# Seven block products in place of eight for the first product of the second layer of an FFT filter, expert and feed-forward kernel

## The chip, the core and the metric

The kernel runs on one core of one Trainium2 chip. Its time is the device time of one execution in microseconds. The kernel before took 3979.79 us, the median of 3 runs (3979.67 to 3984.19).

Five engines work side by side, each through its own list of instructions in order: TensorE (PE in the profile, with PEld for the loading of its stationary operand), VectorE (DVE), ScalarE (ACT), GpSimd (POOL) and SyncE (SP, which here only issues DMAs). They wait for each other by semaphores. Matrix products are written to PSUM, eight banks of 128 x 512 fp32 values, and the other engines read them from there.

## The reference

Three stages follow each other. The first filters `x` (8 batches x 3072 positions x 256 channels) along the positions in the frequency domain. The second sends each of the 24576 tokens through one of 8 experts. The third, the second layer of this document, is a feed-forward layer over all tokens, with `w_in` of 256 x 2048 and `w_out` of 2048 x 256:

```python
def _moe2_ref(x, w_in, w_out) -> np.ndarray:
    h = x @ w_in
    g = h * (1.0 / (1.0 + np.exp(-1.702 * h)))
    return (g @ w_out).astype(np.float32)
```

## The kernel before

The change lies in the last stage, behind `c2.close()`. It works through `nblk` = 48 blocks of 512 tokens. For a block, `load_z` gathers four tiles of 128 tokens x 256 channels by indirect DMAs that POOL issues, `scale_z` multiplies them by a gate value for each token on DVE, and `prep_z` turns them (TensorE transposes, helper `split_t`, L568), so that channels lie on the partitions. The result is split into two fp32r numbers: `xh` is the rounded value (an ACT cast, L573), `xl` the rest (a DVE subtraction, L574). The weights were split in the same way before: `wm[0]`, `wm[1]` (tiles winh, winl) hold `w_in`, and `wm[2]`, `wm[3]` (wouth, woutl) hold `w_out`.

A product of two split matrices is three matmuls: high x high, high x low, low x high. A step `t` of the main loop handles one strip of 128 of the 2048 hidden values of one block:

1. `gemm1` (L583): 6 matmuls 128x128 by 128x512 (two halves of the 256 channels, three each) into one PSUM bank of the pool `ph`, which has four banks.
2. ACT computes the sigmoid of the bank into `sig` (L975), DVE multiplies it with the bank into `gg` (L976).
3. One step later ACT casts `gg` to `hh` (L968) and DVE subtracts to get `hl` (L969).
4. Two steps later `gemm2` (L592) multiplies this strip by its 128 rows of `w_out`: 4 tiles of 128 tokens x 3 matmuls of 256 columns, added up in four PSUM tiles `pz` over the 16 strips of a block.

After strip 15 ACT copies the four `pz` tiles to `zo` (L990) and SP stores them. `load_z` of the block after next stands in step 4 of a block, `scale_z` of the next block in step 8, `prep_z` in steps 9 and 11.

The order is the program's own (`manual_schedule`): each engine executes its instructions in the order in which the Python code writes them, and a pool's buffers decide what has to be waited for. The three lines that set the path of a strip are

```python
                S.copy(hh, gg)
                V.tensor_tensor(hl, gg, hh.bitcast(F32), op=ALU.subtract)
        ...
                p = gemm1(wm[0], wm[1], *xt[j], f, 512)
```

Of the kernel before, what the change touches and what calls it, by code (L numbers as in the profile page):

```python
# [124 lines left out]
def fftconv_moe_moe2(ctx: ExitStack, tc: tile.TileContext, x, ffl, fny, wg, w1, w2, win, wout,  # L125
                     t_sq, t_m2, t_m3, t_sg, t_sm, out):
    nc = tc.nc
# [417 lines left out]

    def open_expert_pools():
        op = lambda n, bufs, **k: tc.tile_pool(name=n, bufs=bufs, reuse_waits="tile", **k)
        pools["xt"] = ctx.enter_context(op("xtp", 2))
        pools["ph"] = ctx.enter_context(op("php", 4, space=PSUM))
        pools["raw"] = c2.enter_context(op("rawp", 1))  # L550
        pools["we"] = c2.enter_context(op("wep", 2))
        pools["m"] = c2.enter_context(op("mp", 2))

# [10 lines left out]
    def split_t(xg, nt, k):  # L564

        p = pools["ph"].tile([128, 4, 128], F32, name="ph", tag="ph")
        for c in range(nt):
            T.transpose(p[:, c, :], xg[:, c, 128 * k:128 * k + 128], eye)  # L568
        return p
# [23 lines left out]
                n += 1  # L593

    def pz_tiles(nt, first):
        return [pools["pz"].tile([128, D], F32, name="pz", tag=f"pz{first + c}") for c in range(nt)]

    raw, wt, xg, xt = {}, {}, {}, {}

# [317 lines left out]
    c2.close()  # L917


    with ExitStack() as c3:  # L920
        gp2 = c3.enter_context(tc.tile_pool(name="gp2", bufs=2, reuse_waits="tile"))
        zg, xt = {}, {}
        nblk = NTOK // 512

        def load_z(j):
# [10 lines left out]
        def scale_z(j):  # L936
            if j >= nblk:
                return
            for c in range(4):
                o = 4 * j + c  # L940
                V.tensor_scalar(zg[j][:, c, :], zg[j][:, c, :], s_all[:, o:o + 1], None, op0=ALU.mult)  # L941

        def prep_z(j, k):
            if j >= nblk:
                return
            if k == 0:
                xt[j] = [pools["xt"].tile([128, 2, 512], F32R, name="xh"), pools["xt"].tile([128, 2, 512], F32R, name="xl")]
            p = split_t(zg[j], 4, k)
            split_out(p, 4, *xt[j], k)
            if k == 1:  # L950
# [5 lines left out]
        scale_z(0)  # L956
        load_z(1)
        prep_z(0, 0)
        prep_z(0, 1)
        gq, hq, pz = {}, {}, {}  # L960
        ns = 16 * nblk
        for t in range(ns + 2):
            j, f = divmod(t, 16)
            if t - 1 in gq:
                gg = gq.pop(t - 1)
                hh = gp2.tile([128, 512], F32R, name="hh", bufs=3)
                hl = gp2.tile([128, 512], F32R, name="hl", bufs=3)
                S.copy(hh, gg)  # L968
                V.tensor_tensor(hl, gg, hh.bitcast(F32), op=ALU.subtract)  # L969
                hq[t - 1] = hh, hl  # L970
            if t < ns:
                p = gemm1(wm[0], wm[1], *xt[j], f, 512)
                sg_ = gp2.tile([128, 512], F32, name="sig")
                gg = gp2.tile([128, 512], F32, name="gg", bufs=3)
                S.activation(sg_, p, AF.Sigmoid, scale=1.702)  # L975
                V.tensor_tensor(gg, p, sg_, op=ALU.mult)  # L976
                gq[t] = gg
                if f == 4:
                    load_z(j + 2)
            if t >= 2:  # L980
                j2, f2 = divmod(t - 2, 16)
                if f2 == 0:
                    pz[j2] = pz_tiles(4, 0)
                hh, hl = hq.pop(t - 2)
                gemm2(hh, hl, wm[2], wm[3], f2, 15, pz[j2])
                if f2 == 15:
                    zo = gp2.tile([128, 4, D], F32, name="zo")
                    b, q = divmod(j2, 6)
                    for c, z in enumerate(pz.pop(j2)):
                        S.copy(zo[:, c, :], z)  # L990
                        if j2 == nblk - 1:
                            nc.sync.dma_start(ov[b][:, 4 * q + c, :], zo[:, c, :])
                    if j2 < nblk - 1:
                        nc.sync.dma_start(ov[b][:, 4 * q:4 * q + 4, :], zo)
                    xt.pop(j2)
            if t < ns and f == 8:
                scale_z(j + 1)
            if t < ns and f in (9, 11):
                prep_z(j + 1, (f - 9) // 2)


_INS = ['x', 'filt_r', 'filt_i', 'moe_w_gate', 'moe_w_output_gate', 'moe_w1', 'moe_w2', 'moe2_w_in', 'moe2_w_out']
# [33 lines left out]
```

## Time and profile before

| what | value |
|---|---|
| median of 3 runs | 3979.79 us (3979.67 to 3984.19) |
| the profiled execution | 3999.94 us, span 3998.1 us |
| mean granted TensorE clock | 0.991 of full speed |
| PE busy | 3903.6 us, 98% of the span |
| second layer, in the span | from about 1776 us to the end |
| blocks x strips in it | 48 x 16 = 768 steps |

The page of the profile shows the share of the span that each engine is busy, the span in 40 slices, the chain of work that ended last, and groups of instructions. A matmul's row is longer than its share of the engine, since matmuls overlap: a row of 283 ns can follow the one before by 120 ns. What a matmul costs in a row of many is read from the distance between two starts, and the same holds for ACT and DVE instructions that do not wait. All times of the trace below are from the profiled execution.

### The profile page before, as it was taken

To read this page: it belongs to the slowest core of one execution; us is meant where nothing else is said; L and a number is where in the kernel's file an instruction comes from. 1 tells how busy PE (TensorE), PEld (TensorE's weight loads), DVE (VectorE), ACT (ScalarE), POOL (GpSimd) and SP (SyncE) were. 2 spreads that over 40 slices of the span, in tenths; PEclk is the share of its full clock that TensorE was granted. 3 is DMA by queue.
4 is the path that set the end of the run, shared out by engine and by line. 5 is a ranking of instruction groups with operands and counts; after the bars stand their busy time and mean duration, and the time that the engine had idled before them with its cause. 6 is when DMAs were issued, how large, how long until landed. Compare 5 with 4: busy or idle time off the path is not lost.

```text
span 3998.1 us, 63838 instructions
## 1 busy us (share of the span) xinstructions
PE 3903.6 (98%) x24892; PEld 3484.0 (87%) x24892; DVE 2344.2 (59%) x4365; ACT 2030.5 (51%) x3940; POOL 749.9 (19%) x935
## 2 busy tenths in 40 slices
PE   6999989999999999999999999999999999999999
PEld 4777768898888899989999999999999999999998
DVE  4667756677777755545555555555555555555554
ACT  3777764444544455544444444444444444444444
POOL 3054556322222222210011000010000010000000
PEclk8999999999999999999999999999999999999999
DMA  9666544445555444430000000000000000000000
GB/s 250 206 205 200 159 141 127 142 149 160 167 159 161 158 153 157 144 104 22 22 23 26 26 23 22 22 25 24 27 22 22 22 27 22 27 22 22 22 22 17
DMA packets 195538, 345.12 MB, mean 86 GB/s; under 512 B 26336, under 2 KB 112992, under 8 KB 194848
## 3 DMA queue, kind: packets, MB, share of 16 engines
q1 hardware_dynamic: 167520, 289.60, 21.9%
q0 software_dynamic: 27296, 51.36, 4.7%
q8 instruction: 197, 3.23, 0.3%
q14 instruction: 109, 0.89, 0.1%
q10 hardware_dynamic: 416, 0.03, 0.0%
HBM read 238.31 MB, written 102.60 MB: 85 GB/s over the span
## 4 chain that ended last, share of the span: by engine, by line
PE 55%; DMA 0%; ACT 0%; DVE 0%; issue 0%
PE pz L592 27%; PE ph L583 27%; PE ph L568 1%; DMA zg<-zs,posz 0%; ACT zo L990 0%; DVE zg L941 0%
## 5 line engine op out<-in xcount | busy, mean ns | idle before, releaser
L592 PE MATMUL pz<-wouth,hl 128*128 128x256 f32 x3072 | 868.9, 283 | 0.0
L592 PE MATMUL pz<-woutl,hh 128*128 128x256 f32 x3072 | 868.0, 283 | 0.0
L592 PE MATMUL pz<-wouth,hh 128*128 128x256 f32 x3072 | 864.8, 282 | 0.0
L976 DVE TENSOR_TENSOR gg<-ph,sig 128x512 f32<-128x512 f32 x768 | 531.0, 691 | 494.3 <-ACT sig L975 492.8
L969 DVE TENSOR_TENSOR hl<-gg,hh 128x512 fp32r<-128x512 f32 x768 | 530.2, 690 | 443.6 <-ACT hh L968 443.6
L975 ACT ACTIVATE sig<-ph 128x512 f32<-128x512 f32 x768 | 458.7, 597 | 586.8 <-PE ph L583 585.1
L968 ACT CAST hh<-gg 128x512 fp32r<-128x512 f32 x768 | 476.9, 621 | 475.2 <-DVE gg L976 418.4
L583 PE MATMUL ph<-xh,winh 128*128 128x512 f32 x1536 | 615.4, 401 | 0.0
L592 PEld LDWEIGHTS pz<-wouth,hh 128*128 128x128 f32 x3072 | 585.8, 191 | 33.3
L592 PEld LDWEIGHTS pz<-woutl,hh 128*128 128x128 f32 x3072 | 585.7, 191 | 30.6
L583 PE MATMUL ph<-xl,winh 128*128 128x512 f32 x1536 | 607.6, 396 | 0.0
L583 PE MATMUL ph<-xh,winl 128*128 128x512 f32 x1536 | 599.3, 390 | 0.0
L592 PEld LDWEIGHTS pz<-wouth,hl 128*128 128x128 f32 x3072 | 585.8, 191 | 0.1
L931 POOL DMA_INDIRECT zg<-zs,posz x192 | 195.8, 1020 | 1927.7 <-PE ph L568 1787.7
L864 ACT ACTIVATE hh<-ph 128x512 fp32r<-128x512 f32 (+1 forms) x464 | 249.3, 537 | 531.9 <-PE ph L583 433.4
L865 DVE SCALAR_TENSOR_TENSOR hl<-ph,hh 128x512 fp32r<-128x512 f32 (+1 forms) x464 | 283.4, 611 | 345.4 <-ACT hh L864 340.2
L592 PE MATMUL pz<-w2h,hh 128*128 128x256 f32 x1584 | 448.6, 283 | 36.8 <-ACT zo L893 36.6
L592 PE MATMUL pz<-w2h,hl 128*128 128x256 f32 x1584 | 446.3, 282 | 0.3 <-DVE hl L865 0.3
L592 PE MATMUL pz<-w2l,hh 128*128 128x256 f32 x1584 | 445.8, 281 | 0.0
L592 PEld LDWEIGHTS pz<-w2h,hh 128*128 128x128 f32 x1584 | 301.0, 190 | 56.2 <-ACT zo L893 41.7
L583 PE MATMUL ph<-xh,w1h 128*128 128x512 f32 (+1 forms) x928 | 348.4, 375 | 0.0
L583 PEld LDWEIGHTS ph<-xh,winl 128*128 128x128 f32 x1536 | 288.9, 188 | 66.1
(197 smaller groups left out, 6228.0 us busy)
## 6 DMA issues: line engine op xcount, KB each, us to landing
w1r<-in_w_dram SPq DMA_DIRECT2D x58, 1024.0 KB
w2r<-in_w_dram SPq DMA_DIRECT2D x58, 1024.0 KB
us<-u SPq DMA_DIRECT2D x96, 256.0 KB
u<-us SPq DMA_DIRECT2D x128, 192.0 KB
out_dram<-zo SPq DMA_DIRECT2D x47, 512.0 KB
yn<-yt SPq DMA_DIRECT2D x90, 256.0 KB
xt<-in_x_dram SPq DMA_DIRECT2D x84, 256.0 KB
zs<-zo SPq DMA_DIRECT2D x41, 512.0 KB
```

Of the source, the lines that this page charges most:

```text
L568: T.transpose(p[:, c, :], xg[:, c, 128 * k:128 * k + 128], eye)
L583: T.matmul(p[:, 0:w], a[:, k, ws], b[:, k, 0:w], start=n == 0, stop=n == 5)
L592: T.matmul(z, a[:, ts], b[:, f, :], start=f == 0 and n == 0, stop=f == last and n == 2)
L864: S.activation(hh[:, 0:w], p[:, 0:w], AF.Relu)
L865: V.scalar_tensor_tensor(hl[:, 0:w], p[:, 0:w], 0.0, hh[:, 0:w].bitcast(F32), op0=ALU.max, op1=ALU.subtract)
L931: G.indirect_dma_start(out=t[:, c, :], out_offset=None, in_=zs, in_offset=bass.IndirectOffsetOnAxis(ap=posz[0][:, o:o + 1].bitcast(U32), a ...
L968: S.copy(hh, gg)
L969: V.tensor_tensor(hl, gg, hh.bitcast(F32), op=ALU.subtract)
L975: S.activation(sg_, p, AF.Sigmoid, scale=1.702)
L976: V.tensor_tensor(gg, p, sg_, op=ALU.mult)
```

## The change

The first product of the layer, for one block, is `h = w_in^T x` with 256 channels. Two strips (a pair `q`; 8 pairs a block) and the two halves of the block's tokens now make a 2 x 2 by 2 x 2 product of blocks: 2 strips x 2 halves of the channels, times 2 halves of the channels x 2 halves of 256 tokens. Before, this took 8 block products (a matmul of 512 columns counts as two); now 7 in Winograd's form of Strassen's method, each of three matmuls 128x128 by 128x256 (`product`, L1014). The first block (j = 0) is still computed by 12 matmuls of 512 columns a pair (`plain`, L1020), while POOL prepares the sums of weight blocks that the method needs (`wsums`); they stay in `sh` and `sl` (4 sums for each of 8 pairs). 47 blocks x 8 = 376 pairs use the seven products.

The sums of token blocks (`t1` to `t4`) are made once a block, by POOL, from copies `rw` of the turned tokens; the casts and subtractions of these follow in pairs 5 to 7. `scale_z` moves from DVE to POOL (from step 8 to pair 2).

The sums of the products are formed in PSUM where they can be: four products add into the left half of one bank (`px`), one behind the other. Between them ACT copies the partial sum out (`snap`, L1067), which the next product of the chain waits for. Two more banks' halves (`py`) take the others. DVE adds the copies to `py` (L1050, L1161). The sigmoid, its product, and the split to `hh` and `hl` then work on `cc` in SBUF, partly in halves of 256. The second product is done in 8 pieces of three matmuls (`chunks`, L1084) which stand between the seven products, two pairs later; its results lie in two banks of 512 columns in place of four tiles, and are copied out by two instructions of 512 columns (L1091). Buffers: `pz` tiles take a whole bank each; two of the four hold the turned tokens; the pool `xt` closes with the experts.

```diff
-        for t in range(ns + 2):
...
-                p = gemm1(wm[0], wm[1], *xt[j], f, 512)
...
-                S.activation(sg_, p, AF.Sigmoid, scale=1.702)
-                V.tensor_tensor(gg, p, sg_, op=ALU.mult)
...
-                gemm2(hh, hl, wm[2], wm[3], f2, 15, pz[j2])
...
+        def wsums(q):
...
+            G.tensor_tensor(af, wv[0][:, q].bitcast(F32), wv[1][:, q].bitcast(F32), op=ALU.add)
...
+            G.tensor_tensor(st[:, 3, :], a12, st[:, 1, :], op=ALU.subtract)
+            yield
+            S.copy(sh[:, q], st)
+            V.tensor_tensor(sl[:, q], st, sh[:, q].bitcast(F32), op=ALU.subtract)
...
+        def product(out, q, a, b, j, start):
...
+            for n, (w, x) in enumerate(((ah, bh), (ah, bl), (al, bh))):
+                T.matmul(out, w, x, start=start and n == 0, stop=n == 2, skip_group_check=True)
...
+        def after(t, s):
...
+            if s == 0:
+                f1 = cc[t][:, 0, :]
+                if t >= np_:
+                    V.tensor_tensor(f1, py.pop(t), sp[t][:, 0:2, :].rearrange("p a b -> p (a b)"), op=ALU.add)
...
+                part(t, 1)
+                g = sig(src)
+                rest_of(t, 1)
+                V.tensor_tensor(f1, src, g, op=ALU.mult)
+            else:
+                part(t, 0)
+                rest_of(t, 0)
...
+            product(x0_, q, (0, 0), 0, j, True)
+            snap(t, 0)
+            after(t - 1, 0)
+            next(g)
+            product(y1, q, (0, 1), 1, j, True)
+            next(g)
+            product(x0_, q, 1, 4, j, False)
+            snap(t, 1)
+            after(t - 1, 1)
+            product(y2, q, 0, 3, j, True)
+            next(g)
+            next(g)
+            product(x0_, q, 2, 5, j, False)
+            snap(t, 2)
+            c22 = cc[t][:, 1, 256:512]
+            V.tensor_tensor(c22, y2, sp[t][:, 2, :], op=ALU.add)
+            next(g)
...
+            next(g)
+            product(x0_, q, (1, 1), 6, j, False)
...
+            a = sig(x0_)
+            b = sig(c22)
+            V.tensor_tensor(cc[t][:, 1, 0:256], x0_, a, op=ALU.mult)
+            V.tensor_tensor(c22, c22, b, op=ALU.mult)
+            px.pop(t)
+            next(g)
+            next(g)
+            product(y2, q, 3, 2, j, False)
```

In this diff `g` is the iterator over the 8 pieces of the second product of pair t - 2, and `part` and `rest_of` are the cast to `hh` and the subtraction to `hl` of one strip.

TensorE, one step of the second layer before, from its first product into its second (`ph` and `pz` are the PSUM tiles of the two products):

```order
L583 MATMUL ph<-xh,winh 128x512
L583 MATMUL ph<-xl,winh 128x512
L583 MATMUL ph<-xh,winl 128x512
L592 MATMUL pz<-wouth,hh 128x256 [waits Activation_49]
L592 MATMUL pz<-woutl,hh 128x256
L592 MATMUL pz<-wouth,hl 128x256 [waits DVE_49]
```

TensorE now, in the middle of a pair: the third product of the chain in `px`, two pieces of the second product, and the fourth product of the chain (`sh`, `sl` are sums of weight blocks):

```order
L1014 MATMUL ph<-xh,sh 128x256 [waits Activation_49]
L1014 MATMUL ph<-xl,sh 128x256
L1014 MATMUL ph<-xh,sl 128x256
L1084 MATMUL pz<-wouth,hh 128x256
L1084 MATMUL pz<-woutl,hh 128x256
L1084 MATMUL pz<-wouth,hl 128x256
L1084 MATMUL pz<-wouth,hh 128x256
L1084 MATMUL pz<-woutl,hh 128x256
L1084 MATMUL pz<-wouth,hl 128x256
L1014 MATMUL ph<-xh,winh 128x256 [waits Activation_49]
L1014 MATMUL ph<-xl,winh 128x256
L1014 MATMUL ph<-xh,winl 128x256
```

All matmuls of a pair now have 256 columns, and a product waits for ACT's copy with two pieces between it and the product whose sum is copied.

ACT at the end of a block before (`sig`, then `hh` of the strip, then the copies of the block's result to `zo`):

```order
L975 ACTIVATE sig<-ph 128x512 [waits PE_49,Activation_49]
L968 CAST hh<-gg 128x512 [waits DVE_49]
L975 ACTIVATE sig<-ph 128x512 [waits PE_49,Activation_49]
L968 CAST hh<-gg 128x512 [waits DVE_49]
L990 COPY zo<-pz 128x256 [waits DMAHW2_49,PE_49]
L990 COPY zo<-pz 128x256 [waits PE_49] x3
```

ACT now, one pair, the one in which a block's result is copied out (`sp` is the copy of a partial sum):

```order
L1067 COPY sp<-ph 128x256 [waits PE_49]
L1037 CAST hh<-cc 128x512 [waits DVE_49]
L1030 ACTIVATE sig<-cc 128x512 [waits DVE_49,Activation_49]
L1067 COPY sp<-ph 128x256 [waits PE_49]
L1037 CAST hh<-cc 128x512 [waits DVE_49]
L1091 COPY zo<-pz 128x512 [waits DMAHW6_49,PE_49]
L1067 COPY sp<-ph 128x256 [waits PE_49]
L1030 ACTIVATE sig<-ph 128x256 [waits PE_49,Activation_49]
L1030 ACTIVATE sig<-cc 128x256 [waits DVE_49]
L1091 COPY zo<-pz 128x512 [waits PE_49]
```

ACT's list for a pair has grown from four instructions of 512 columns (two steps) to eight; the first copy to `zo` stands ahead of the third copy of a partial sum.

POOL before, in the second layer (the four gathers of a block, and the first of the next):

```order
L931 DMA zg<-zs,posz 128x256 [waits DMASW6_49,DVE_49,PE_49]
L931 DMA zg<-zs,posz 128x256 [waits DMASW7_49]
L931 DMA zg<-zs,posz 128x256 [waits DMASW0_49]
L931 DMA zg<-zs,posz 128x256 [waits DMASW1_49]
L931 DMA zg<-zs,posz 128x256 [waits DMASW2_49,DVE_49,PE_49]
```

POOL now, one block:

```order
L939 DMA zg<-zs,posz 128x256 [waits PE_49]
L939 DMA zg<-zs,posz 128x256 x3
L949 TENSOR_SCALAR zg<-zg,s_all 128x256 [waits DMASW6_49]
L949 TENSOR_SCALAR zg<-zg,s_all 128x256 [waits DMASW7_49]
L949 TENSOR_SCALAR zg<-zg,s_all 128x256 [waits DMASW0_49]
L949 TENSOR_SCALAR zg<-zg,s_all 128x256 [waits DMASW1_49]
L983 TENSOR_TENSOR rw<-rw 128x256 [waits DVE_49,Activation_49]
L984 TENSOR_TENSOR rw<-rw 128x256 [waits Activation_49,Pool_49]
L985 TENSOR_TENSOR rw<-rw 128x256
L986 TENSOR_TENSOR rw<-rw 128x256 [waits Pool_49]
```

The four multiplications and the four sums of a block are added behind the gathers, on an engine that had only the gathers.

## Rows read from the trace of the kernel before

**Rows 1.** The page: busy time, share of the span, instructions.

```profile
PE 3903.6 (98%) x24892; PEld 3484.0 (87%) x24892; DVE 2344.2 (59%) x4365; ACT 2030.5 (51%) x3940; POOL 749.9 (19%) x935
```

**Rows 2.** Busy time by stretch: stretch, length, then busy us (instructions).

```profile
3000.00:3100.00 100.00, 100.00 (x644) 90.94 (x644) 53.56 (x86) 46.08 (x82) 8.20 (x8) 1.00 0.07 22
```

**Rows 3.** Timeline of PE: start, duration, line, tiles. One step.

```profile
3003.24 0.40 PE L583 MATMUL ph<-xh,winh 128*128 128x512 f32 x1
...
3004.63 0.28 PE L592 MATMUL pz<-wouth,hh 128*128 128x256 f32 x1
...
3006.06 0.40 PE L583 MATMUL ph<-xh,winh 128*128 128x512 f32 x1
```

**Rows 4.** Groups by line, 1900 to 3990 us: busy, mean ns | idle before.

```profile
L976 DVE TENSOR_TENSOR gg<-ph,sig 128x512 f32<-128x512 f32 x727 | 502.6, 691 | 467.9 <-ACT sig L975 466.4 <-issue 1.5
L969 DVE TENSOR_TENSOR hl<-gg,hh 128x512 fp32r<-128x512 f32 x728 | 502.6, 690 | 419.7 <-ACT hh L968 419.7
L968 ACT CAST hh<-gg 128x512 fp32r<-128x512 f32 x728 | 452.0, 621 | 449.1 <-DVE gg L976 395.4 <-issue 53.8
...
L990 ACT COPY zo<-pz 128x256 f32<-128x256 f32 x180 | 56.4, 383 | 0.0
...
L573 ACT CAST xh<-ph 128x512 fp32r<-128x512 f32 x90 | 52.9, 588 | 108.8 <-PE ph L568 108.8
```

**Rows 5.** Timeline of the experts' last block, products of 256 columns.

```profile
1769.74 0.28 PE L583 MATMUL ph<-xh,w1h 128*128 128x256 f32 x1
...
1770.34 0.28 PE L583 MATMUL ph<-xh,w1l 128*128 128x256 f32 x1
...
1770.65 0.38 ACT L864 ACTIVATE hh<-ph 128x256 fp32r<-128x256 f32 x1 [1.04 <-PE ph L583]
...
1771.07 0.42 DVE L865 SCALAR_TENSOR_TENSOR hl<-ph,hh 128x256 fp32r<-128x256 f32 x1 [1.00 <-ACT hh L864]
```

**Rows 6.** Timeline: ACT and DVE instructions one behind the other.

```profile
3951.36 1.25 ACT L990 COPY zo<-pz 128x256 f32<-128x256 f32 x4
...
3009.52 0.59 ACT L573 CAST xh<-ph 128x512 fp32r<-128x512 f32 x1 [1.21 <-PE ph L568]
...
3010.00 0.63 ACT L968 CAST hh<-gg 128x512 fp32r<-128x512 f32 x1
...
3010.14 0.69 DVE L574 TENSOR_TENSOR xl<-ph,xh 128x512 fp32r<-128x512 f32 x1 [1.11 <-ACT xh L573]
...
3010.75 0.68 DVE L969 TENSOR_TENSOR hl<-gg,hh 128x512 fp32r<-128x512 f32 x1
```

**Rows 7.** Timeline of the first stage: DVE beside POOL, then alone.

```profile
53.65 0.69 DVE L239 TENSOR_TENSOR yv<-pv,ff 128x512 f32<-128x512 f32 x1
...
53.70 1.04 POOL L198 TENSOR_TENSOR ff<-ff,sg 128x512 f32<-128x512 f32 x1 [5.69 <-DVE ff L195]
...
54.26 1.02 DVE L254 TENSOR_TENSOR w<-w,ff 128x512 f32<-128x512 f32 x1
...
157.42 0.69 DVE L255 TENSOR_TENSOR yv<-yv,w 128x512 f32<-128x512 f32 x1
...
160.08 0.69 DVE L254 TENSOR_TENSOR w<-w,ff 128x512 f32<-128x512 f32 x1
```

**Rows 8.** POOL by line, the whole span, and two gathers in time.

```profile
L198 POOL TENSOR_TENSOR ff<-ff,sg 128x512 f32<-128x512 f32 x16 | 16.6, 1041 | 61.1 <-DVE ff L195 61.0
...
L761 POOL COPY iw<-sq 128x128 f32<-128x128 f32 x2 | 0.5, 286 | 0.1
...
1778.18 0.95 POOL L931 DMA_INDIRECT zg<-zs,posz  x1 [53.13 <-SPq L906]
1779.43 0.95 POOL L931 DMA_INDIRECT zg<-zs,posz  x1 [0.30 <-issue]
```

**Rows 9.** Timeline: ACT's cast and the first matmul of the layer.

```profile
1785.66 0.58 ACT L573 CAST xh<-ph 128x512 fp32r<-128x512 f32 x1 [8.89 <-PE ph L568]
...
1786.29 0.80 PE L583 MATMUL ph<-xh,winh 128*128 128x512 f32 x1
```

More of the change, by code (lines that the diff above doesn't have):

```diff
@@ L595, in pz_tiles @@
     def pz_tiles(nt, first):
-        return [pools["pz"].tile([128, D], F32, name="pz", tag=f"pz{first + c}") for c in range(nt)]
+        return [pools["pz"].tile([128, 512], F32, name="pz", tag=f"pz{first + c}")[:, 0:D] for c in range(nt)]
     raw, wt, xg, xt = {}, {}, {}, {}
@@ L934, in load_z, with scale_z @@
             zg[j] = t
-        def scale_z(j):
+        def scale_z(j, eng):
             if j >= nblk:
@@ new lines, in product, with plain @@
+        def product(out, q, a, b, j, start):
+            ah, al = (wv[0][:, q, a[1], a[0], :], wv[1][:, q, a[1], a[0], :]) if isinstance(a, tuple) else \
+                (sh[:, q, a, :], sl[:, q, a, :])
+            bh, bl = xo[j][0][:, b, :], xo[j][1][:, b, :]
+            for n, (w, x) in enumerate(((ah, bh), (ah, bl), (al, bh))):
+                T.matmul(out, w, x, start=start and n == 0, stop=n == 2, skip_group_check=True)
+        def plain(out, q, i, j):
+            n = 0
+            for k in range(2):
+                for w, x in ((0, 0), (0, 1), (1, 0)):
+                    T.matmul(out, wv[w][:, q, k, i, :], xo[j][x][:, 2 * k:2 * k + 2, :].rearrange("p a t -> p (a t)"),
+                             start=n == 0, stop=n == 5)
+                    n += 1
@@ new lines, in fftconv_moe_moe2, with sig, part @@
+        ov = out.rearrange("(b p n) d -> b p n d", n=N2, p=N1)
+        px, py, cc, sp, hq, zq, zo = {}, {}, {}, {}, {}, {}, {}
+        def sig(src):
+            t = gp2.tile([128, 512], F32, name="sig")
+            w = src.shape[-1]
+            S.activation(t[:, 0:w], src, AF.Sigmoid, scale=1.702)
+            return t[:, 0:w]
+        def part(t, i):
+            if i == 1:
+                hq[t] = [gp2.tile([128, 2, 512], F32R, name=n) for n in ("hh", "hl")]
+            S.copy(hq[t][0][:, i, :], cc[t][:, i, :])
@@ new lines, in snap, with chunks @@
+        def snap(t, i):
+            if i == 0:
+                sp[t] = gp2.tile([128, 3, 256], F32, name="sp")
+            S.copy(sp[t][:, i, :], px[t][:, 0:256])
+        def chunks(t):
+            if not 0 <= t < npair:
+                while True:
+                    yield
+            j, q = divmod(t, np_)
+            h, l = hq.pop(t)
+            if q == 0:
+                zq[j] = [pools["pz"].tile([128, 512], F32, name="pz", tag=f"pz{b}") for b in range(2)]
+            for b in range(2):
+                z = zq[j][b]
+                for i in (1, 0):
+                    for c in range(2):
+                        ts = slice(256 * b + 128 * c, 256 * b + 128 * c + 128)
+                        for n, (a, w) in enumerate(((h, 2), (h, 3), (l, 2))):
+                            T.matmul(z[:, 256 * c:256 * c + 256], a[:, i, ts], wm[w][:, 2 * q + i, :],
+                                     start=q == 0 and i == 1 and c == 0 and n == 0,
+                                     stop=q == np_ - 1 and i == 0 and n == 2, skip_group_check=True)
+                        if q == np_ - 1 and i == 0 and c == 1:
+                            if b == 0:
+                                zo[j] = gp2.tile([128, 4, D], F32, name="zo")
+                            bq, r = divmod(j, 6)
+                            S.copy(zo[j][:, 2 * b:2 * b + 2, :], z.rearrange("p (c d) -> p c d", c=2))
+                            if j == nblk - 1:
+                                nc.sync.dma_start(ov[bq][:, 4 * r + 2 * b:4 * r + 2 * b + 2, :],
+                                                  zo[j][:, 2 * b:2 * b + 2, :])
+                            elif b == 1:
+                                nc.sync.dma_start(ov[bq][:, 4 * r:4 * r + 4, :], zo.pop(j))
+                        yield
+            while True:
+                yield
@@ L954, in fftconv_moe_moe2 @@
         load_z(0)
         S.activation(gap, gap, AF.Sigmoid)
[L956 removed]
+        scale_z(0, V)
         load_z(1)
[L958 to L961, printed above, removed]
[L962 to L999 removed]
```

114 lines of the change are left out of this document (105 added, 9 removed).

## Prediction

> **What bounds the kernel now.** I read the page's busy times first, then the busy times of a stretch of the second layer, then PE's timeline there, then the groups by line. PE is busy for 98% of the span [rows 1], and in a stretch of 100 us of the second layer for all 100, with DVE at 53.6 and ACT at 46.1 [rows 2]. Since matmul rows overlap, "busy" alone could hide slack, so the starts decide: in one step six matmuls of 512 columns take 4.63 - 3.24 = 1.39 us and twelve of 256 columns take 6.06 - 4.63 = 1.43 us, and the next step follows at once [rows 3]. A 512 costs 0.2317 us, a 256 costs 0.1192. Against this ACT and DVE wait for each other half of the time [rows 4]: the idle time before `sig`, `gg`, `hh` and `hl` costs nothing now. So the layer is bound by the number and width of matmuls, and every nanosecond taken from PE there is a gain as long as ACT and DVE still keep up.
>
> **Term 1, the matmuls.** A pair of strips had 12 matmuls of 512 and 24 of 256; it gets 21 + 24 of 256. The second product stays: 24 of 256. The first goes from 12 x 0.2317 = 2.780 us to 21 x 0.1192 = 2.503. That is 0.277 us a pair, and for the 47 x 8 = 376 pairs 104 us. Columns alone would promise an eighth of 2.78, 0.35 us; narrow matmuls cost a little more for each column. The price of 0.1192 is not only that of the second product: in the experts' last block first products of 256 columns start five intervals in 0.60 us [rows 5], 0.12 each. Transposes are as many as before.
>
> **Does the rest keep up?** The new point is the chain in `px`: four products add into one bank half, and before each of the last three ACT must have copied the sum out. PE's pair has 15 places of three matmuls, 0.358 us each, 5.36 us in all: 1 first product of the chain, 2 piece of the second product, 3 `y1`, 4 piece, 5 second of the chain, 6 `y2`, 7 and 8 pieces, 9 third of the chain, 10 and 11 pieces, 12 fourth, 13 and 14 pieces, 15 the end of `y2`. I walk ACT and DVE through it by hand, in us from the pair's start:
>
> - Place 1: its last matmul starts at 0.24, and ACT reads a 256 product 0.31 after that (1770.34 to 1770.65, [rows 5]): first copy at 0.55. An ACT instruction behind a copy of 256 starts 0.29 after it ((1.25 - 0.38) / 3, [rows 4, 6]): `hh` of the pair before at 0.84.
> - That cast takes 0.62 [rows 4], and DVE follows 0.03 later [rows 5]: `hl` at 1.49. The product with the sigmoid starts 0.61 behind it [rows 6], at 2.10 (its sigmoid, 0.52 behind `hh`, is ready at about 2.0), and ends 0.69 later [rows 4]: `hh` of the other strip at 2.82.
> - ACT's next one comes 0.52 after a cast (0.48 after one of 0.59, [rows 6], plus 0.03): 3.34. This is the third copy, but its sum stands only at 8 x 0.358 + 0.55 = 3.41. It takes 0.38 [rows 4], and PE starts 0.05 after ACT's end (1786.24 to 1786.29, [rows 9]): the fourth product may start at 3.84. Its place is 11 x 0.358 = 3.93.
>
> So the chain fits, with 0.09 us there and 0.07 before the third copy: a margin of 0.16. The other two copies are earlier (0.98 for a place at 1.43; 2.41 for one at 2.86), and place 15 (5.01) waits for DVE's reading of `y2`, over at about 4.55. By throughput there is room: DVE has four instructions of 512 at 0.61 and three of 256 at 0.34 (0.42 [rows 5], less the same 0.08), 3.5 us; ACT has about 3.0; both of 5.36. Casts and subtractions of `prep_z` in pairs 5 to 7 stand behind the third copy and fall into this room. `scale_z` leaves DVE, where it was hidden.
>
> **Term 2, the copy out.** In one pair of every block the first copy to `zo`, now 512 wide, stands ahead of the third copy on ACT: it delays that from 3.41 to 3.34 + 0.48 = 3.82, and the fourth product from 3.93 to 4.25. 0.32 x 47 = 15 us given back. Before, these copies cost nothing (idle 0.0 before them, [rows 4], and PE did not wait).
>
> **Term 3, POOL beside DVE.** No row shows POOL's elementwise work in the second layer, but the first stage shows both engines together: DVE's L254, which reads two SBUF tensors, takes 1.02 us while POOL's L198 runs and 0.69 alone, while L239, which reads PSUM and SBUF, keeps 0.69 beside POOL [rows 7]. One such meeting costs 0.33. `hl` and the product with the sigmoid now read two SBUF tensors and lie on the chain. When does POOL run? The second turned copy `rw` of pair 4 is ready at about 4.8; three sums of 256 at half of 1.04, 0.52 [rows 8], end about 0.6 into pair 5; four gathers at 1.25 (1778.18 to 1779.43, [rows 8]) end 0.3 to 0.7 into pair 6; then the four multiplications run. Their price is not in the trace: between 0.29 (a copy of 128 columns) and 1.04 (two inputs of 512), and I take about 0.5. They then lie over 1.49 and 2.10 of the chain. One or two meetings, 0.33 to 0.66, less the margin of 0.16: I take 0.34 a block, 16 us. Ends: 0, when the multiplications are short and past by 1.49, and 2 x 0.55 - 0.16 = 0.94 a block, 44 us, when each of the two instructions waits for a whole one of POOL's.
>
> The Trainium skill has a rule on this, in "SBUF — State Buffer", section "Who interferes with whom": a DVE instruction with two SBUF inputs and a GpSimd instruction that reads SBUF exclude each other, and whichever starts first holds the shared ports to its end. Rows 7 agree: L254 starts at 54.26, POOL ends at 54.74, and L254 ends 0.54 later. By the rule in full, at both places, the sum would be the third case below; by the row it is the 16 us.
>
> **Term 4, the edges.** In the first block POOL sums weights, 1.04 + 4 x 0.29 = 2.2 us a pair beside a step pattern with much slack; at the end the last pair's `hl` is waited for a little. 3 us together, 0 to 8.
>
> Sum: -104 + 15 + 16 + 3 = -70 us. The profiled execution (span 3998.1, time 3999.94) would come to about 3930. It is 20 us above the median of the runs, so taken from the median: 3979.8 - 70 = 3910 us.
>
> **Rivals.**
>
> 1. POOL does not hit the chain. For it: the multiplication has one tensor input and may be far shorter than half of L198. Against: four of them in a row have to end in 0.8 us. -104 + 15 + 3 = -86: 3894.
> 2. The forecast: 3910, with 3900 to 3925 for one to two partial meetings.
> 3. Each of the two DVE instructions on the chain waits for a whole POOL instruction: -104 + 15 + 44 + 3 = -42: 3938.
> 4. The other side: the chain of ACT and DVE becomes the bound in every pair. Its place is the wait before the fourth product. For it: a margin of 0.16 us on a path of six instructions, none of whose new forms (sigmoid and cast of `cc` in SBUF, a copy of a half bank beside matmuls) is in the trace. Against: the cast from SBUF costs 0.62 where the one from PSUM costs 0.59 [rows 4], so forms differ by 0.03. It gives back all from 0.16 + 70 / 376 = 0.35 us of extra length, 0.06 for each of the six. With 0.1 each: (0.6 - 0.16) x 376 = 165, so 4075.
> 5. The change does not do what it says: if a 256 product cost 2.780 / 21 = 0.132, nothing would be won, 3980 + 34 = 4014 with the terms given back. Rows 3 and 5 both speak against it.
>
> **How the numbers follow.** Case 2 has 0.40, case 1 has 0.25, case 3 has 0.16, a chain that is late by less than the gain (3925 to 3970) has 0.06, case 4 has 0.10, and what comes out at no change or like case 5 has 0.03. Faster by over 0.2% (8 us, about what a measurement of this kernel can tell from no change) is cases 1 to 3 and most of the late chain: 0.85. Slower: case 4 and part of the last, 0.11; within 0.2%: 0.04. The range starts at 3884, case 1 with 10 us less for the copy out and the edges, and ends at 3968, case 3 with a chain late by 0.08 us in each pair (30 us); below lies about 0.07, above 0.13.
>
> **What would show it.** On PE's timeline of a middle pair, 45 starts 0.119 apart and a pair of 5.36 us with no idle time; this fails if products start 0.13 apart (case 5). In pair 1 of a block one gap of 0.3 us before the first matmul that reads a plain weight into `px`, released by ACT's copy `sp`; in pair 6 a gap of 0.2 to 0.5 at the same place, with an `hl` or a product row of DVE longer than 0.9 beside a POOL multiplication. If that gap stands in every pair, case 4 holds. DVE should be near 65% and ACT near 56% busy by starts, more by rows. The forecast would be wrong if POOL's rows are longer than 1 us, if DVE's two-input instructions are stretched in other pairs as well, or if a block's eight pairs, without its transposes, take much more than 8 x 5.36 + 0.32 + 0.34 = 43.5 us (45.1 before for 16 steps of 2.82).

## The result

The changed kernel takes 3924.71 us (median of 4 runs, 3921.42 to 3934.65) against 3981.99 for the kernel before beside it (3979.67 to 3989.59): a ratio of 0.9857 with a 95% interval of 0.9834 to 0.988, 57 us less. Measured again later it was 3926.15 against 3984.78, 0.9851 (0.9836 to 0.9866). The forecast was 3910 in a range of 3884 to 3968. The profiled execution took 3934.65 us (span 3932.7), 65.4 us less span than the one of before.

### The profile after

The page's busy times, which answer to [rows 1]:

```profile
PE 3835.5 (98%) x28276; PEld 3598.6 (92%) x28276; DVE 2719.8 (69%) x5407; ACT 2512.1 (64%) x5544; POOL 1188.5 (30%) x1351
```

The same 100 us as in [rows 2]; columns are the stretch, its length, then busy us of PE, PEld, DVE, ACT and POOL with their instructions, the granted clock, the DMA share and GB/s:

```profile
3000.00:3100.00 100.00, 99.75 (x831) 99.35 (x831) 71.69 (x135) 71.11 (x162) 25.74 (x24) 1.00 0.08 27
```

PE is still the bound, with a quarter of a microsecond idle in 100 us. DVE and ACT went from about half to 0.71: the slack is smaller, and POOL is at work in a quarter of the time.

Timeline of pair 0 of a block, from its start at 3034.43 to the next pair's at 3039.83, rows of ACT, DVE and the first matmuls of two products (start, duration). They answer to [rows 3] and to the walk by hand:

```profile
3034.43 0.28 PE L1014 MATMUL ph<-xh,winh 128*128 128x256 f32 x1
...
3034.99 0.37 ACT L1067 COPY sp<-ph 128x256 f32<-128x256 f32 x1 [0.40 <-PE ph L1014]
...
3035.26 0.62 ACT L1037 CAST hh<-cc 128x512 fp32r<-128x512 f32 x1
...
3035.92 0.69 DVE L1041 TENSOR_TENSOR hl<-cc,hh 128x512 fp32r<-128x512 f32 x1 [0.24 <-ACT hh L1037]
...
3036.53 0.69 DVE L1058 TENSOR_TENSOR cc<-cc,sig 128x512 f32<-128x512 f32 x1
3037.25 0.62 ACT L1037 CAST hh<-cc 128x512 fp32r<-128x512 f32 x1 [0.44 <-DVE cc L1058]
3037.88 0.37 ACT L1067 COPY sp<-ph 128x256 f32<-128x256 f32 x1
...
3038.39 0.29 PE L1014 MATMUL ph<-xh,winh 128*128 128x256 f32 x1
...
3039.83 0.28 PE L1014 MATMUL ph<-xh,winh 128*128 128x256 f32 x1
```

From the pair's start the six instructions begin at 0.56, 0.83, 1.49, 2.10, 2.82 and 3.45 us, where the walk had 0.55, 0.84, 1.49, 2.10, 2.82 and 3.41; the fourth product starts at 3.96, which is its place: 33 matmuls of 0.12 stand ahead of it. The pair takes 5.39 to 5.40 us.

Groups by line, 1900 to 3920 us (busy us, mean ns | idle before), which answer to [rows 4] and [rows 8]:

```profile
L1041 DVE TENSOR_TENSOR hl<-cc,hh 128x512 fp32r<-128x512 f32 x727 | 510.5, 702 | 392.8 <-ACT hh L1037 384.7
L1037 ACT CAST hh<-cc 128x512 fp32r<-128x512 f32 x727 | 451.4, 621 | 160.1 <-DVE cc L1058 160.1
...
L1058 DVE TENSOR_TENSOR cc<-cc,sig 128x512 f32<-128x512 f32 x364 | 250.0, 687 | 0.1
...
L949 POOL TENSOR_SCALAR zg<-zg,s_all 128x256 f32<-128x256 f32 x176 | 220.6, 1263 | 1.6
...
L1091 ACT COPY zo<-pz 128x512 f32<-128x512 f32 x90 | 52.5, 583 | 0.0
L986 POOL TENSOR_TENSOR rw<-rw 128x256 f32<-128x256 f32 x45 | 41.9, 932 | 0.0
```

`hl` and the product with the sigmoid are 0.702 and 0.687 us on average, little over the 0.690 of `hl` before, in spite of POOL. POOL's own instructions are long: 1.26 us for a multiplication, 0.93 for the last of a block's four sums and 0.75 for the others.

The mean length of each pair of a block, from PE's timeline (start of a pair to the start of the next, 47 blocks), in us; before, a pair is two steps. Pair 0 is without that of block 1 (6.19 us, counted with the first block), pairs 3 and 4 are without those of the last block, which has no transposes:

| pair | after | why |
|---|---|---|
| 0, 2, 7 | 5.394 | steady, 45 matmuls |
| 1 | 5.780 | copy to `zo` |
| 3, 4 | 5.827 each | four transposes each, as before |
| 5, 6 | 5.439 each | POOL beside DVE |
| block | 44.49 | before: 45.99 |

So a block is 1.49 us shorter, 70 us over 47 blocks. First block and end give back 7.4, which leaves 62.9 in the layer (2208.0 to 2145.1 us from the start of its first product to the start of its last matmul). Of the rest of the 65.4, 2.7 us lie ahead of the layer, where the work is the same (it starts at 1783.6 in place of 1786.3), and 0.2 are lost behind it.

Pair 1, PE, PEld (weight loads) and ACT, at the fourth product:

```profile
3043.17 0.58 ACT L1091 COPY zo<-pz 128x512 f32<-128x512 f32 x1
...
3043.64 0.38 ACT L1067 COPY sp<-ph 128x256 f32<-128x256 f32 x1
...
3044.07 0.19 PEld L1014 LDWEIGHTS ph<-xh,winh 128*128 128x128 f32 x1 [0.33 <-ACT sp L1067]
3044.07 0.39 PE L1014 MATMUL ph<-xh,winh 128*128 128x256 f32 x1
3044.29 0.28 PE L1014 MATMUL ph<-xl,winh 128*128 128x256 f32 x1
3044.41 0.28 PE L1014 MATMUL ph<-xh,winl 128*128 128x256 f32 x1
```

The copy to `zo` holds the third partial sum, the product starts 0.285 late, and then its second matmul comes 0.22 later instead of 0.12: a stall costs 0.10 beyond its own length. The weight load stands at the same start as the matmul, so it had not been done ahead. The Trainium skill, "TensorE: Matmul & The Clock Gate", section "Architectural detail: the array is 16× 32×32, not 1× 128×128", says that PE's queue can pull weight loads ahead of matmuls in flight. Where nothing stalls the trace agrees, with a load about 0.12 us ahead of its matmul; this row shows that a load behind a semaphore wait was not ahead.

POOL beside DVE, at the start of pair 5 and in pair 6 (two views of one timeline), which answer to [rows 7]:

```profile
3018.02 0.75 POOL L985 TENSOR_TENSOR rw<-rw 128x256 f32<-128x256 f32 x1
3018.12 0.92 DVE L1174 TENSOR_TENSOR cc<-cc,sig 128x256 f32<-128x256 f32 x1
3018.71 0.93 POOL L986 TENSOR_TENSOR rw<-rw 128x256 f32<-128x256 f32 x1
...
3025.11 0.82 DVE L1041 TENSOR_TENSOR hl<-cc,hh 128x512 fp32r<-128x512 f32 x1
...
3025.53 4.14 POOL L949 TENSOR_SCALAR zg<-zg,s_all 128x256 f32<-128x256 f32 x3
...
3025.85 0.68 DVE L1058 TENSOR_TENSOR cc<-cc,sig 128x512 f32<-128x512 f32 x1
```

A product of 256 columns takes 0.92 beside two of POOL's sums (0.42 at 3034.66 in pair 0, without POOL), `hl` 0.82. But the product L1058, right behind `hl`, has its usual 0.68 with POOL's multiplication open beside it, and that multiplication is the long one (1.71 us; the shortest of 176 is 0.91). It looks as if DVE's next instruction came first and POOL waited; no run shows this by itself.

The first block, waits of 1783 to 1833 us (waiting engine and line, releaser: us in total, times, longest), and stretches as above:

```profile
ACT sh L1004 <- POOL ws L1002: 13.1, 4, 4.8
...
PE pz L1084 <- DVE hl L1041: 1.5, 3, 0.8
```

```profile
1783.50:1790.00 6.50, 6.50 (x18) 4.83 (x18) 3.08 (x5) 2.82 (x6) 5.57 (x9) 0.58 0.17 53
...
1800.00:1810.00 10.00, 7.82 (x44) 6.41 (x45) 5.16 (x7) 4.40 (x9) 8.91 (x13) 0.97 0.01 2
1810.00:1832.00 22.00, 22.00 (x136) 20.02 (x136) 17.03 (x23) 12.25 (x23) 17.93 (x25) 0.93 0.00 1
```

ACT's `sh` waits for POOL's sums of weights, and stands in ACT's list ahead of the `hh` that PE needs. PE idles 2.2 us in 1800 to 1810; then the granted clock is 0.93 on average, so a part of the stretch ran at 1.2 in place of 2.4 GHz. The layer also starts at a low clock, and for longer than it did before:

```profile
1786.20:1790.00 3.80, 3.80 (x12) 2.72 (x11) 1.38 (x2) 1.19 (x3) 2.88 (x4) 0.63 0.36 104
```

That is the start of the layer in the kernel before. What the clock lacks of 1.00, times the stretch, is 2.7 us now (0.42 of 6.50) and 1.4 before (0.37 of 3.80), an estimate of what it costs.

### The profile page after: what moved, and what is told of

Read it like the earlier page. It is cut to its first block, busy times and chain, and to the rows that moved or that the text cites. A ratio compares the mean times of both kernels' runs of the same rounds, so it can differ in the third digit from the quotient of the medians.

```text
span 3932.7 us, 73157 instructions
## 1 busy us (share of the span) xinstructions
PE 3835.5 (98%) x28276; PEld 3598.6 (92%) x28276; DVE 2719.8 (69%) x5407; ACT 2512.1 (64%) x5544; POOL 1188.5 (30%) x1351
## 4 chain that ended last, share of the span: by engine, by line
PE 49%; ACT 2%; DVE 2%; issue 1%; POOL 1%; POOLq 0%
PE pz L1084 25%; PE ph L1014 23%; PE pt L956 1%; DVE hl L1041 1%; ACT sp L1067 1%; DVE cc L1058 1%; ACT hh L1037 1%; ACT zo L1091 1%; POOL zg L939 0%; POOL af L997 0%; DVE sl L1005 0%; POOL zg L949 0%; POOL ws L999 0%; ACT sh L1004 0%; POOL ws L1000 0%
## 5 line engine op out<-in xcount | busy, mean ns | idle before, releaser
L1084 PE MATMUL pz<-wouth,hh 128*128 128x256 f32 x3072 | 876.0, 285 | 1.0 <-ACT hh L1037 1.0
L1084 PE MATMUL pz<-wouth,hl 128*128 128x256 f32 x3072 | 868.5, 283 | 1.5 <-DVE hl L1041 1.5
L1084 PE MATMUL pz<-woutl,hh 128*128 128x256 f32 x3072 | 868.1, 283 | 0.0
L1041 DVE TENSOR_TENSOR hl<-cc,hh 128x512 fp32r<-128x512 f32 x768 | 542.2, 706 | 412.5 <-ACT hh L1037 404.1
L1037 ACT CAST hh<-cc 128x512 fp32r<-128x512 f32 x768 | 476.8, 621 | 177.5 <-DVE cc L1058 174.9
L1084 PEld LDWEIGHTS pz<-wouth,hl 128*128 128x128 f32 x3072 | 587.3, 191 | 2.2 <-DVE hl L1041 2.1
L1084 PEld LDWEIGHTS pz<-wouth,hh 128*128 128x128 f32 x3072 | 587.5, 191 | 2.0 <-ACT hh L1037 1.4
L1084 PEld LDWEIGHTS pz<-woutl,hh 128*128 128x128 f32 x3072 | 587.4, 191 | 0.4
L1067 ACT COPY sp<-ph 128x256 f32<-128x256 f32 x1128 | 419.1, 372 | 240.5 <-PE ph L1014 223.3
L658 POOL DMA_INDIRECT xg<-yn,ids x198 | 198.7, 1003 | 769.1 <-PE ph L568 678.9
L1014 PE MATMUL ph<-xh,sh 128*128 128x256 f32 x1504 | 425.9, 283 | 0.5 <-ACT sp L1067 0.4
L1014 PE MATMUL ph<-xh,sl 128*128 128x256 f32 x1504 | 425.6, 283 | 0.0
L1014 PE MATMUL ph<-xl,sh 128*128 128x256 f32 x1504 | 425.6, 283 | 0.0
L1030 ACT ACTIVATE sig<-cc 128x256 f32<-128x256 f32 x752 | 392.2, 521 | 3.7 <-ACT hh L1037 0.3
L983 POOL TENSOR_TENSOR rw<-rw 128x256 f32<-128x256 f32 x47 | 35.2, 749 | 1160.7 <-ACT rw L977 1160.7
```

The costliest lines, as they stand in the source:

```text
L658: i = G.indirect_dma_start(out=t[:, c, :], out_offset=None, in_=yn if j >= NE else yn[0:BE * SEQ, :], in_offset=bass.IndirectOffsetOnAxis( ...
L1014: T.matmul(out, w, x, start=start and n == 0, stop=n == 2, skip_group_check=True)
L1030: S.activation(t[:, 0:w], src, AF.Sigmoid, scale=1.702)
L1037: S.copy(hq[t][0][:, i, :], cc[t][:, i, :])
L1041: V.tensor_tensor(l[:, i, :], cc[t][:, i, :], h[:, i, :].bitcast(F32), op=ALU.subtract)
L1067: S.copy(sp[t][:, i, :], px[t][:, 0:256])
```

## Experiments

All times are medians; a ratio is to runs of the kernel before on the same chip. The kernel before took 3939.63 on the chip of the first four experiments (copy late, scale on DVE, longer chain, wide products; their layers start at 1725 to 1730 us, so the stage ahead is shorter there, and undisturbed pairs have the same lengths), 3984.78 on that of the next four, and 3987.54 on the last. "Layer" is from the start of its first product to the start of its last matmul in the profile, "block" the mean as in the table above.

| run | us | ratio | interval | block | layer |
|---|---|---|---|---|---|
| after again | 3926.15 | 0.9851 | 0.9836 to 0.9866 | 44.50 | 2145.3 |
| copy late | 3858.27 | 0.9796 | 0.978 to 0.9812 | 44.11 | 2127.2 |
| scale on DVE | 3872.96 | 0.9828 | 0.9811 to 0.9844 | 44.44 | 2141.1 |
| wide products | 3939.24 | 0.9999 | 0.9989 to 1.0008 | | 2208.4 |
| all three | 3904.72 | 0.9795 | 0.9782 to 0.9808 | 44.07 | 2123.2 |
| gathers late | 3909.99 | 0.9813 | 0.9797 to 0.983 | | 2125.1 |

Single executions: the longer chain 4096.11, more POOL 4271.29, narrow second product 4321.87.

### Is the gain the matmuls? Twelve wide products in every block

```diff
-            if j == 0:
+            if True:
                 plain(px[t], q, 1, j)
...
-                if t >= np_:
+                if False:
                     V.tensor_tensor(f1, py.pop(t), ...)
```

No seven products, no sums of blocks. Pairs, the pieces of the second product (four and four), the wide copies out and the multiplications on POOL stay.

> The changed kernel with its first block's way of computing in all blocks: 12 matmuls of 512 columns a pair and no sums of blocks, but with the changed order, the two wide copies out, the pieces of the second product and the multiplication on POOL. Theory (the gain is that of fewer matmul columns): 8 pairs of 5.64 and the transposes, 46.0 us a block as in the kernel before, so 3975 to 3990, within 10 us of it. Rival (order and copies out bring the gain, seven products or eight do not matter): about 3925.

Ratio 0.9999, and a layer of 2208.4 us for 2208.0. The frame (pairs, pieces, two-bank results, multiplications on POOL) neither wins nor costs more than 0.1%; the gain comes from the seven products, and the give-backs belong to what comes with them.

### Term 2: the copy to `zo` behind the third partial sum

```diff
-                            S.copy(zo[j][:, 2 * b:2 * b + 2, :], z.rearrange(...))
+                            held.append((zo[j], z))
...
             snap(t, 2)
+            for o, z in held:
+                S.copy(o[:, 0:2, :], z.rearrange("p (c d) -> p c d", c=2))
```

> The first of a block's two copies to zo stands behind ACT's third copy of a partial sum instead of ahead of it; nothing else changes. Theory (the copy out holds up the third copy, and the fourth product of the chain waits for it): pair 1 of a block falls from 5.780 to 5.39 us, the 47 gaps of 0.39 us are gone, 18 us less than the changed kernel. Rival (PE waits in pair 1 for something else that comes at the same time, such as the bank of the second product): the gap stays or moves to pair 2, and the time with it.

Timeline of pair 1 (started at 3014.73):

```profile
3018.17 0.37 ACT L1067 COPY sp<-ph 128x256 f32<-128x256 f32 x1
...
3018.43 0.59 ACT L1166 COPY zo<-pz 128x512 f32<-128x512 f32 x1
...
3018.68 0.29 PE L1014 MATMUL ph<-xh,winh 128*128 128x256 f32 x1
```

The copy to `zo` and the third copy of a partial sum have changed places, and the fourth product stands at 3.96, its place. Pair 1 falls from 5.780 to 5.402, the layer by 17.9 us. Term 2 is shown, with its 0.10 for the restart: 0.387 x 47 = 18.2.

### Term 3: the multiplications back on DVE

```diff
-                scale_z(j + 1, G)
...
             V.tensor_tensor(c22, y2, sp[t][:, 2, :], op=ALU.add)
+            if q == 2:
+                scale_z(j + 1, V)
```

> The multiplication of a block's tokens by their gate values goes back to DVE (behind the addition that reads y2, in pair 2; in the first block at the start of pair 2); the sums stay on POOL. Theory (POOL's multiplications stretch DVE's hl in pair 6, POOL's sums stretch the product of c22 in pair 5): pair 6 falls from 5.439 to 5.39, pair 5 stays at 5.44, 2 us in all; in the first block POOL reaches its weight sums about 5 us earlier, so PE's gaps of 4 us there shrink to under 1 and the granted clock stays at 1.00 between 1800 and 1832: 3 to 6 us. Together 5 to 8 us less. Rival (POOL beside DVE costs nothing, pairs 5 and 6 are longer by the casts and subtractions of prep_z): pairs 5 and 6 both stay at 5.44, and pair 2 gets longer by up to 1 us (47 us).

Group by line, 1900 to 3860 us:

```profile
L949 DVE TENSOR_SCALAR zg<-zg,s_all 128x256 f32<-128x256 f32 x172 | 48.7, 346 | 0.0
```

On DVE a multiplication takes 0.346 us against 1.263 on POOL, and is hidden (pair 2 keeps 5.393). Pair 6 falls from 5.439 to 5.399, pair 5 to 5.419, and the first block with the pair behind it by 1.6 us: the layer is 4.1 shorter, less than the 5 to 8 expected, since the first block gave 1.6 in place of 3 to 6. So the multiplications on POOL cost 2.5 us in 47 blocks, not 16. What stays in pair 5 goes with POOL's sums: there the product of 256 columns still takes 0.91 us beside them.

### The opposite: POOL busy in every pair

```diff
+            for _ in range(4):
+                G.tensor_tensor(pad[:, 2, :], pad[:, 0, :], pad[:, 1, :], op=ALU.add)
             x0_, y1, y2 = px[t][:, 0:256], py[t][:, 0:256], py[t][:, 256:512]
```

> The changed kernel with four more POOL sums of two inputs of 256 columns in every pair, on a tile that nothing else uses. Theory (POOL and a DVE instruction with two SBUF inputs exclude each other, whoever started first runs to its end, so each of hl and the product with the sigmoid can wait for what is left of one POOL instruction): on the average 0.2 to 0.3 us for each of the two, less the 0.1 us the chain has to spare and plus 0.1 us for a stalled product, so pairs of 5.7 to 6.0 us and a whole over 4000. Rival (POOL gives way, DVE goes on, and POOL's rows are what gets longer): pairs of 5.39 to 5.50.

Timeline of a pair 0 (started at 3017.44):

```profile
3018.92 1.56 DVE L1041 TENSOR_TENSOR hl<-cc,hh 128x512 fp32r<-128x512 f32 x1 [0.53 <-ACT hh L1037]
3019.17 3.85 POOL L1149 TENSOR_TENSOR pad<-pad 128x256 f32<-128x256 f32 x4
...
3020.41 1.22 DVE L1058 TENSOR_TENSOR cc<-cc,sig 128x512 f32<-128x512 f32 x1
...
3022.60 0.39 PE L1014 MATMUL ph<-xh,winh 128*128 128x256 f32 x1 [1.05 <-ACT sp L1067]
```

In this pair `hl` goes to 1.56 us and the product to 1.22, each about doubled (0.98 and 1.05 on average over the layer), and the fourth product is 1.2 us late. By their place in the block pairs take 5.83 to 7.89 us on average, more than the 5.7 to 6.0 expected. POOL works in order, so its added sums slip: in one block eight of them start in pair 6 and none in pair 4, and pair 4 keeps its 5.83. The Trainium skill, "SBUF — State Buffer", section "Who interferes with whom", has a two-input DVE instruction contend with a GpSimd instruction that reads SBUF; this run bears it out. The third term was small all the same, since in the changed kernel POOL meets the chain in little more than pairs 5 and 6.

### Rival 4: the chain

```diff
             product(x0_, q, 2, 5, j, False)
+            for _ in range(2):
+                S.copy(gp2.tile([128, 256], F32, name="pad", bufs=1), sp[t][:, 0, :])
             snap(t, 2)
```

> Two more ACT copies of 256 columns in every pair, ahead of the third copy of a partial sum; their result is not used. They are 0.31 us apart, 0.62 us on the chain. Theory (the chain from the first copy to the third has about 0.1 us before the third copy and 0.1 behind it to spare): an undisturbed pair grows from 5.39 by 0.62 - 0.21 = 0.41 to 5.80 us, the whole by some 140 us (pair 1 grows by the full 0.62), slower than the kernel before. Rival (ACT is busy for only two thirds and the copies hide): pairs stay at 5.39, and only pair 1 grows.

Timeline of a pair 0 (started at 3004.71):

```profile
3008.05 0.84 ACT L1160 COPY pad<-sp 128x256 f32<-128x256 f32 x2
...
3008.79 0.36 ACT L1067 COPY sp<-ph 128x256 f32<-128x256 f32 x1
...
3009.21 0.39 PE L1014 MATMUL ph<-xh,winh 128*128 128x256 f32 x1 [0.38 <-ACT sp L1067]
3009.43 0.28 PE L1014 MATMUL ph<-xl,winh 128*128 128x256 f32 x1
```

The two copies stand 0.43 apart (0.31 was expected; that it comes from the buffer they share is not shown), so they lengthen ACT's list by 0.74. The third copy moves from 3.44 to 4.09, 0.65, so ACT had 0.10 to spare; the fourth product moves from 3.96 to 4.50, 0.55, so PE had another 0.10. With 0.10 for the restart the pair is 0.64 longer, 6.03 in place of the 5.80 expected: 0.74 - 0.20 + 0.10. The margin that the walk put at 0.16 is 0.20. Rival 4's mechanism is real; its point was not reached.

### What a 256 costs: a second product of 128 columns

```diff
-                            T.matmul(z[:, 256 * c:256 * c + 256], a[:, i, ts], wm[w][:, 2 * q + i, :],
+                            T.matmul(z[:, 256 * c:256 * c + 128], a[:, i, ts], wm[w][:, 2 * q + i, 0:128],
```

Half of each result stays zero, set by DVE.

> The second product with 128 columns in place of 256 (half of the output is left out, as zeros), all else as in the changed kernel. Read from the distance between two starts inside a piece of three matmuls. Theory (a run of matmuls of 256 columns, each with its own weights, goes at the pace of the weight loads, 0.12 us): the distance stays at 0.11 to 0.12, and the pair at 5.3 us or more. Rival (the columns set the pace): 0.06 inside a piece; the pair then falls to 4.6 to 5.2 us, held by ACT's and DVE's chain.

PE in two pieces and the product behind them, with two of PE's weight loads (PEld):

```profile
3053.70 0.22 PE L1086 MATMUL pz<-wouth,hh 128*128 128x128 f32 x1
3053.76 0.27 PE L1086 MATMUL pz<-woutl,hh 128*128 128x128 f32 x1
3053.81 0.19 PEld L1086 LDWEIGHTS pz<-wouth,hl 128*128 128x128 f32 x1
3053.87 0.28 PE L1086 MATMUL pz<-wouth,hl 128*128 128x128 f32 x1
3053.92 0.19 PEld L1086 LDWEIGHTS pz<-wouth,hh 128*128 128x128 f32 x1
3053.98 0.28 PE L1086 MATMUL pz<-wouth,hh 128*128 128x128 f32 x1
...
3054.32 0.33 PE L1014 MATMUL ph<-xh,sh 128*128 128x256 f32 x1
3054.49 0.28 PE L1014 MATMUL ph<-xl,sh 128*128 128x256 f32 x1
```

Only the first narrow one is cheap (0.06); the others start 0.11 apart, and the 256 behind them takes 0.17: six narrow ones and a 256 in 0.79 us, where seven of 256 take 0.84. Half the columns in six of seven save 6%. So at 128 columns the column count does not set the pace. The weight loads go at 0.11 here, each 0.05 behind the start of a matmul, where in the stream of 256s a load starts with the matmul ahead of it, within 0.01 (3034.44 for 3034.43 in the changed kernel). That fits the theory that the loads set the pace at 128 columns; whether they do at 256 it does not show. The whole time says nothing (the zeroing makes PE wait in pair 2, and the clock falls to 0.93 on average), and the steady pair's 5.235 us, for 5.3 or more expected, is held by the chain too: the fourth product shows the 0.22 restart of a stall. The starts alone carry this.

### All three edits

Copy late, multiplications on DVE, and in the first block the gathers for block 2 in pair 6 instead of pair 1, with the first weight sums ahead of those for block 1.

```diff
+        ws0 = wsums(0)
+        next(ws0)
         load_z(1)
...
-            if q == 1:
+            if q == (1 if j else 6):
                 load_z(j + 2)
```

> Both edits of before together (the first copy to zo behind the third copy of a partial sum; the multiplication by the gate values on DVE), and in the first block POOL starts the first weight sums ahead of the second block's gathers and issues the third block's gathers in pair 6 in place of 1. Theory: 18 us of the copy, 2.5 us of pairs 5 and 6, and in the first block, from the first product to the second block's first one, 49.1 falls to about 43, as PE no longer waits for the sums: together some 26 us less than the changed kernel, a ratio to the kernel before of about 0.979. Rival (the first block waits for something else than POOL): it stays at 47 or more and the gain is 21 us.

This beats both kernels: 0.9795 of before, 21.4 us under the changed kernel on the same chip. But the layer is 22.1 shorter than in after again where 26 were expected, no more than the first two edits give (17.9 + 4.1). The third moved its loss:

| us | first block | block 1, pair 0 | pair 1 |
|---|---|---|---|
| after | 48.29 | 6.19 | 6.07 |
| all three | 42.65 | 9.97 | 5.39 |
| gathers late | 42.71 | 6.09 | 10.97 |

Stretches of the kernel with all three:

```profile
1821.00:1823.00 2.00, 1.03 (x7) 0.63 (x6) 1.78 (x3) 0.18 (x1) 1.92 (x4) 1.00 0.00 0
1823.00:1826.00 3.00, 1.53 (x9) 1.33 (x10) 2.53 (x5) 3.00 (x7) 2.25 (x3) 0.83 0.15 44
1826.00:1832.00 6.00, 6.00 (x43) 6.00 (x42) 3.80 (x8) 3.04 (x8) 1.89 (x2) 0.80 0.23 66
```

PE idles 2.4 us at the border of the blocks. In the 9 us of the last two stretches the granted clock is 0.83 and 0.80 on average, so a part of them ran at 1.2 in place of 2.4 GHz, which costs up to 1.7 more (0.17 of 3 us and 0.20 of 6).

### Gathers for block 2 at the start of block 1

```diff
+            if t == np_:
+                load_z(2)
-            if q == (1 if j else 6):
+            if q == 1 and j:
                 load_z(j + 2)
```

> The version with all three edits, in which the gathers for block 2 are moved once more: out of pair 6 of the first block, where POOL makes the last weight sums behind them, to the start of block 1, where POOL has nothing else to do. Theory: in the version with three edits TensorE stands for 2.4 us around 1822 because `sh` on ScalarE waits 4.3 us for POOL's sums of pair 7, which stand behind four gathers of about 1.35 us, and then the granted clock falls to about 0.8 up to 1832 and costs another 1.7 us. Without gathers there, the wait and the low clock go: the first block takes 43 to 44 us in place of 47.2, and the layer is 3 to 4 us shorter. Rival: the weight sums themselves are too slow for a pair (about 5.5 us of POOL in a pair with VectorE beside it); then the stall is the same or stands in another pair and the first block takes 46 us or more. Whole time in either case 3900 to 3906 on the chip of the second call, hardly to be told apart by the time alone.

Timeline of ACT in pairs 0 and 1 of block 1:

```profile
1824.84 0.41 ACT L1030 ACTIVATE sig<-cc 128x256 f32<-128x256 f32 x1
1828.80 0.37 ACT L1067 COPY sp<-ph 128x256 f32<-128x256 f32 x1 [3.56 <-remote]
```

The stall at the border went, as the theory had it (42.71 and what pair 0 takes over a steady one, 0.70, make 43.4 us in place of 47.2), but a new one stands in pair 1: ACT idles 3.56 us before its first copy of a partial sum and DVE 1.65 before its next sum, both released by what the trace calls remote, an event that it puts down to no instruction it shows. Of the eight gathers issued from the start of the block, some run at that time. Whether they cause it, and whether other executions show it, stays open. This version is not better: layer 2125.1 against 2123.2.

### The changed kernel again

> The changed kernel once more, on the chip and between the runs of the others of this call, so that they can be compared with it. All theories: a ratio to the kernel before of 0.983 to 0.988, and pairs of 5.393 us.

Ratio 0.9851, steady pair 5.393, layer 2145.3. The layer repeats within 0.3 us; runs of one kernel differ ahead of it (it starts at 1773.8 here and at 1783.6 in the first profile).

## Why the prediction was right, and where it was not

**The bound and the gain (term 1).** Right in kind: PE's matmuls were the bound, and wide products in the new frame give ratio 0.9999. The size was 93 us, not 104: a steady pair is 5.393, not 5.363. The step that was off is the price of 0.1192. That mean [rows 3] holds the first starts behind the 512s, which come early; in a stream of 256s alone each takes 0.12, and 45 x 0.0007 is the missing 0.03 us a pair. The second source of the prediction, five intervals in 0.60 us [rows 5], had the right price.

**The chain.** Right to 0.04 us at each of the six instructions, with a margin of 0.20 for 0.16 (the run with the longer chain). Sums of starts and distances from rows of before were enough for it, even for forms that no row showed.

**Term 2.** The wait, its place and its length (0.285 for 0.32) were right; the restart of 0.10 behind a stall was not seen. 18.2 us for 15.

**Term 3.** Mis-sized: 4.3 us for 16. The durations were too short (0.5 for a multiplication that takes 1.26, outside the bounds of 0.29 and 1.04, 0.52 for sums of 0.75 and 0.93) and the meeting too dear. The gathers stretch too (1.19 us on average, [rows 8] has 0.95), so the multiplications begin at 1.9 in pair 6, when `hl` at 1.49 is over by half; the product behind it keeps its length, and the margin takes most of the rest. Pair 5, which I had not named, pays as much; more than half of that stays when only the sums are left on POOL.

**Term 4.** 7.4 us for 3. The first block takes 49.1 us to the steady start of block 1 where 41.8 would do (44.7 before, less two steps' second products at 1.43 that now come later). The step that failed is "a step pattern with much slack": POOL's weight sums stand in front of ACT's list, and a stall is paid a second time in clock. They are also longer than the 2.2 us a pair of the prediction: the means of the five sums (1.33, 0.66, 0.51, 0.52 and 0.46) add up to 3.5. Of the 7.3 us too much, PE's idle time from 1790 to 1810 is 2.5, the clock behind the stall about 1.7, and the longer start at a low clock about 1.3; the rest is not resolved. The tail is 3.0 longer, and 2.9 of that are those moved products.

In sum: -92.9 + 18.2 + 4.3 + 7.4 = -63.0 in the layer for -70, against 62.9 measured. That the sum is this near is in part luck: 11 us too much gain in term 1 and 12 us too much loss in term 3 cancel.

The medians of all runs differ by 57 and 59, 4 to 6 less than the layer. On the chip of the first four experiments nothing of this is lost: copy late and scale on DVE lie 81.4 and 66.7 us under the kernel before, and their layers are 80.8 and 66.9 shorter. On that of the next four, the version with all three edits loses 4.7 (80.1 for 84.8). So the loss goes with the chip. The stage ahead is where runs of one kernel differ, but the kernel before was traced on one chip alone, and where the loss lies is not shown.

Two of the signs that the prediction set for being wrong did appear: POOL's rows are longer than 1 us, and DVE's two-input instructions are stretched in another pair too. They did not decide, since the margin took most of it; the third sign, a block without its transposes, came out at 43.6 us for 43.5 (44.49 less the 0.87 that pairs 3 and 4 take over a steady pair).

The time lies between the forecast and rival 3 (3938), but not for rival 3's reason: POOL's part is nearer to rival 1's, and the rest of the miss is the price of a matmul, the restart and the first block. Rivals 3 and 5 fell by the rows of `hl` and by the starts of 0.12, rival 4 by the walk.

## What to carry to other kernels

When engines work in order, walk the chain by hand from starts and distances of the old trace; here it hit to 0.04 us and named pair 1, the one that stalls (and pair 6, which hardly does). Price a matmul from a stream of its own kind, not from a mean behind wider ones, and add a restart to each stall of TensorE. Before giving GpSimd work to free VectorE, look what VectorE would take for it (0.35 us here against 1.26), and what stands in line behind the result.

## What the runs showed of the hardware that was not expected

- A stall of PE before a product costs 0.10 us beyond its length: the matmul behind the first one starts 0.222 later in place of 0.12, in pair 1 and in the run with the longer chain alike.
- Halving the columns of six matmuls from 256 to 128, each with its own weight load, shortens them and the 256 behind them from 0.84 to 0.79 us.
- A gather's row on POOL grows from 0.95 to up to 1.5 us, and a multiplication's from 0.91 to 1.73, in the same kernel.
- PE idle for 2.4 us within 5 was followed by a low granted clock, 0.80 on average over the 6 us behind it, though PE was then busy throughout.
